# The late form of attention starts at unit 16 instead of unit 24, inside the first batch

## The chip, the cores and the metric

The kernel runs on one core of one Trainium2 chip. Its time is the device time of one execution in microseconds; lower is better. The core has five engines that work side by side, each in its own fixed order: PE (TensorE, matrix products), DVE (VectorE), ACT (ScalarE), POOL (GpSimd) and SP (SyncE, which issues nearly all DMAs here). An instruction starts when the ones before it in its engine's queue have started and what it waits for is done, so an engine can stand still behind one instruction that waits.

## The reference

Sliding-window attention with ALiBi-like distances, then a feed-forward block with a rational activation:

```
scores = q @ k^T / sqrt(64); keep = key < 8  or  0 <= query - key < 96
bias   = -slope(head) * distance                  # slopes 2^-1 .. 2^-8
attn   = softmax(keep ? scores + bias : -1e9) @ v # 4 batches, 8 heads, 768 rows, 64 wide
x      = attn, heads side by side                 # 3072 tokens x 512
h      = x @ w_in                                 # 512 -> 2048
g      = (a0 + a1 h + a2 h^2 + a3 h^3) / (1 + |b0| |h| + |b1| h^2 + 1e-6)
out    = g @ w_out                                # 2048 -> 512
```

## The kernel before

**Units and pairs.** The tokens go in 12 chunks of 256, a chunk is two tiles of 128 rows, a batch is six tiles. A *unit* is one tile and one pair of heads, so a chunk has 8 units, a batch 24, and the program 96 (`u`, or `t` for the step of the loop that starts it). A tile sees itself and the tile before it (window 96) and the first 8 keys of the batch. A *pair* `f` is a chunk's FFN on two blocks of 128 hidden columns: 8 pairs per chunk, 96 in all. Step `t` starts unit `t` and the pair `f` whose `turn(f)` falls on it: the FFN lags the attention by 10 steps at first and by 13 later (EARLY_LAG, LAG).

**The plain form** (units below PLAIN = 24). q and k are transposed on PE (L390); ACT scales q into `qz` (L403) and copies k into `kF` (L405), which holds two tiles of keys, the own and the former. The scores (L434) are full fp32 products; on PE each such product appears as two records. DVE adds the mask and takes the minimum (L453), ACT exponentiates (L463), DVE forms the reciprocal sums (L468, L470), POOL normalizes (L479). The probabilities are transposed on PE (L492) and copied out by ACT, from unit 21 on by DVE (L493). L541 multiplies with v; `st_x` splits the result into a rounded part and a rest (L570 ACT, L571 DVE).

**The late form** (units from PLAIN on). q and k of two units are moved by a DMA into a ring of one buffer, `moved` (L148, tiles `mv`), and transposed with a rounding type (L384). ACT writes the rounded half and DVE the rest of keys and queries into `kq` (L416, L417), two DMAs build the swapped query `qT` (L421, L422), and the score takes four faster matmuls (L439). The normalized probabilities are transposed in 32x32 blocks by DVE (L504), written to DRAM and read back by five DMAs (L507, L515). Here a unit's score comes two steps after its start and its product with v eight steps after; v is loaded at step `t` instead of `t - 4`.

**FFN.** The first chunk (pairs 0 to 7) uses fp32 weights (`full`, L264 and L343). The later ones use weights split in two (`hi`, `w_lo`; L272 and L348, three matmuls for each product). `split_w` makes the splits at the pairs 5 to 14 (SPLITS; L223, L224) on DVE, ACT and POOL. Weights arrive in steps 0 to 16 (WSCHED), are decoded by L203, L207, L208, L210. `h` has two buffers in PSUM, so the first matmul of pair f + 2 waits for the last reader of pair f, L304 on DVE. The elementwise steps of a pair are L296 to L298, L312, L313, L327 on ACT, L303, L304, L317 to L319 on DVE, L305 and L328 on POOL.

**What sets the order.** Each group of instructions gets a number, `base + 1000 * step + PRI[...]`, and a list scheduler puts the instructions of every engine into a fixed order by it. At `t == PLAIN` the pool `early` (kF, qz, three of the raw weight buffers) is closed and the pool `late` (kq, kG, halves, moved, turned, qT) takes its place in SBUF, so its first writes wait for the last readers of the old one. In the kernel before, this falls on the end of the first batch, where tile 0 of the next batch needs no earlier keys.

Of the kernel before, what the change touches and what calls it, by code (L numbers as in the profile page):

```python
# [9 lines left out]
F32 = mybir.dt.float32  # L10
FR = mybir.dt.float32r
# [3 lines left out]
AF = mybir.ActivationFunctionType  # L15
ALU = mybir.AluOpType
PSUM = bass.MemoryType.PSUM

P = 128
G = 8  # L20
# [6 lines left out]
LAG = 13  # L27
EARLY_LAG = 10
# [4 lines left out]
EARLY = 21  # L33


PLAIN = 24
DIVIDED = 8

WSCHED = {0: [(1, 1)], 1: [(1, 0)], 3: [(1, 3)], 4: [(1, 2)], 6: [(0, 0)], 7: [(0, 1)], 8: [(1, 5)], 9: [(1, 4)],
          10: [(0, 2)], 11: [(0, 3)], 12: [(0, 4), (1, 6)], 13: [(1, 7)], 14: [(0, 5)], 15: [(0, 6)], 16: [(0, 7)]}  # L40

SPLITS = {4: 0, 5: 2, 6: 4, 7: 8, 8: 12, 9: 16, 10: 19, 11: 22, 12: 25, 13: 28, 14: 32}

# [64 lines left out]
def tile_kernel(ctx: ExitStack, tc: tile.TileContext, q, k, v, n_global, n_local,  # L108
                w_in, w_out, ca, cb, out):
    nc = tc.nc  # L110
    B, H, S, D = q.shape
# [6 lines left out]
    NPAIR = H // 2  # L118
    UPC = 2 * NPAIR
    FPC = NFT // 2  # L120
# [4 lines left out]
    pl = SimpleNamespace(tmps=TMPS, gbufs=GBUFS, split=False)  # L125
# [5 lines left out]
    def unit(u):  # L131
        c, j = divmod(u, UPC)
        t, p = divmod(j, NPAIR)
        b, i = divmod(2 * c + t, NT)
        return c, t, p, b, i
# [238 lines left out]
    def blocks_of(x, i):  # L374
        return x if i else x[..., 0, :]

    def st_qkT(u):
        p = unit(u)[2]
        if u >= PLAIN:
            tk = pl.ps_t.tile([P, 2, 2, P], FR, tag="t", name=f"tk{u}")  # L380
# [15 lines left out]
    def st_qkE(u):  # L396
        c, t, p, b, i = unit(u)
        tk = tqk.pop(u)
        if u < PLAIN:
            qz = pl.qz[:, u % 3]  # L400
# [26 lines left out]
    def st_score(u):  # L427
# [3 lines left out]
        for x in range(2):  # L431
            h = 2 * p + x
            if u < PLAIN:
                nc.tensor.matmul(out=blocks_of(s_ps[:, x], i), lhsT=qT[:, x, :], rhs=blocks_of(pl.kF[:, p], i),  # L434
# [3 lines left out]
            for z, lhsT in enumerate((pl.kq[:, h, 2, :], qT[:, x, :])):  # L438
                nc.tensor.matmul(out=s_ps[:, x], lhsT=lhsT, rhs=rhs, start=(z == 0), stop=(z == 1))  # L439
        if 1 <= i < NT - 1 and u < PLAIN:  # L440
            nc.gpsimd.tensor_copy(out=pl.kF[:, p, i % 2, 0:G], in_=pl.kGF[:, p, :])
# [4 lines left out]
        def mask(x):  # L446
            m0, m = (mask0, masks) if u < PLAIN or x == 0 else (pl.half0, pl.halves)
            return m0 if i == 0 else m[:, 0:2, :] if i % 2 else m[:, 1:3, :]
        pr = pl.att.tile([P, 2, 2, P], F32, tag="prob", name=f"pr{u}")
        st = stats[:, u % 4]  # L450
        for x in range(2):
            h = 2 * p + x
            nc.vector.tensor_tensor_reduce(  # L453
                out=blocks_of(pr[:, x], i), in0=blocks_of(s_ps[:, x], i), in1=mask(x),
                scale=-(2.0 ** -(h + 1 if u < PLAIN else 2 * p + 1)), scalar=3e38, op0=ALU.add, op1=ALU.min, accum_out=st[:, x:x + 1])
        prob[u] = (pr, st)
# [120 lines left out]
    def windowed(lates):  # L577
# [32 lines left out]
        base = tc.cur_priority  # L610

        def halve_masks():
            for m, full_m in ((pl.halves, masks), (pl.half0, mask0)):
                nc.vector.tensor_scalar(out=m, in0=full_m, scalar1=0.5, scalar2=None, op0=ALU.mult)

        def turn(f):
            return f + EARLY_LAG + (LAG - EARLY_LAG) * min(max(f - 2 * FPC, 0), FPC) / FPC

        f = -1
        for t in range(NU + LAG + F2 + 1):  # L620
            step = int(turn(f + 1)) <= t
            f += step
            when = {True: 1000 * turn(f), False: 1000 * t}
            pri = {True: PRI_A if f < FPC else PRI, False: PRI_A if t < FPC + EARLY_LAG else PRI}

            def on(name, fn, u, *args, ffn=False, more=0):
                if 0 <= u < NU:
                    tc.cur_priority = int(base + when[ffn] + pri[ffn][name] + more)
                    fn(u, *args)

            def ffn(name, fn, u, *args):
                if step:
                    on(name, fn, u, *args, ffn=True)
# [15 lines left out]
            for u in behind(1):  # L649
                on("score", st_score, u)  # L650
                on("soft", st_soft, u)
                on("sums", st_sums, u)
            if t == PLAIN:
                scope.close()
                pl.late = lates.enter_context(tc.tile_pool(name="late", bufs=1))
                pl.kq = pl.late.tile([P, H, 3, P], FR, name="kq")
                pl.kG = pl.late.tile([P, H, G], FR, name="kG")
                pl.halves = pl.late.tile([P, 3, P], BF16, name="halves")
                pl.half0 = pl.late.tile([P, P], BF16, name="half0")
                tc.cur_priority = base + 1000 * t  # L660
                halve_masks()
                on("split", st_move, t)
            ffn("ffn1a", st_ffn1, f, 0)
            if t < PLAIN or t % 2 == 0:
# [138 lines left out]
    with ExitStack() as es:  # L803
        pl.far = es.enter_context(tc.tile_pool(name="far", bufs=1, space=bass.MemoryType.DRAM))
        pl.ldp = es.enter_context(tc.tile_pool(name="ldp", bufs=2))
        pl.att = es.enter_context(tc.tile_pool(name="att", bufs=2))
        pl.ffn = es.enter_context(tc.tile_pool(name="ffn", bufs=2))
        pl.ps_h = es.enter_context(tc.tile_pool(name="ps_h", bufs=2, space=PSUM))
        pl.ps_o = es.enter_context(tc.tile_pool(name="ps_o", bufs=2, space=PSUM))
        pl.ps_r = es.enter_context(tc.tile_pool(name="ps_r", bufs=1, space=PSUM))  # L810
        pl.ps_t = es.enter_context(tc.tile_pool(name="ps_t", bufs=3, space=PSUM))
        with ExitStack() as lates:
            windowed(lates)
# [53 lines left out]
```

## Time and profile before

| | |
|---|---|
| median of 3 runs | 733.48 us (733.4 to 734.27) |
| the profiled execution | 732.77 us, span 730.9 us, mean granted clock 0.995 |
| busy in the span | PE 706.0 us (97%), PE weight loads 608.0 (83%), DVE 604.1 (83%), ACT 577.1 (79%), POOL 457.5 (63%) |
| chain that ended last | PE 83%, DVE 6%, ACT 5%, DMA 2%, issue 2% |

The span runs from the first to the last instruction of the profiled execution; the execution's own time is 1.87 us longer. Busy time is a union: where two rows of an engine overlap, the time counts once, while the durations in a row's own column run into the next row. A matmul's row is longer than the time until the next matmul starts, since they are pipelined. The chain of waits is followed back from the last instruction, and each of its pieces lasts until the next piece begins. A few matmul records can be missing.

### The profile page before, as it was taken

Reading aid. Unit: us, or ns where it says so; the run is one execution under the profiler, and the core shown is the slowest. Engines: PE = TensorE matmul, PEld = TensorE weight load, DVE = VectorE, ACT = ScalarE, POOL = GpSimd, SP = SyncE. Lnnn points to the kernel's source line nnn. Section 1 sums busy time; section 2 is a strip of 40 time slices with the busy share of each in tenths; the row PEclk is TensorE's granted clock in tenths of the full one; section 3 lists DMA queues with packets and bytes.
Section 4 is the critical chain, followed back from the end, with each engine's and each line's share of the span. In section 5 each row is a group of like instructions: output and inputs, shape, how many; then the busy total and the mean of one; then the engine's idle time right before and its main releaser. Section 6 shows DMA issues by size and latency. Waiting matters only on the chain.

```text
span 730.9 us, 14868 instructions
## 1 busy us (share of the span) xinstructions
PE 706.0 (97%) x4762; PEld 608.0 (83%) x4762; DVE 604.1 (83%) x1508; ACT 577.1 (79%) x1304; POOL 457.5 (63%) x504
## 2 busy tenths in 40 slices
PE   5898999999999999999999999999999999999996
PEld 4575666788978889988988998998998998988894
DVE  5789966789889898888889889898889988875664
ACT  6798576977988788888887878887888878865764
POOL 3275986767567675665566657665667666754441
PEclk9999999999999999999999999999999999999998
DMA  9987210114564654645536455665346454421001
GB/s 265 294 278 215 89 23 22 52 23 105 157 166 133 200 154 130 182 141 154 142 111 181 140 136 166 173 183 137 98 121 197 138 160 129 118 88 30 30 1 34
DMA packets 139899, 96.76 MB, mean 132 GB/s; under 512 B 84260, under 2 KB 124196, under 8 KB 139812
## 3 DMA queue, kind: packets, MB, share of 16 engines
q1 hardware_dynamic: 138608, 95.20, 45.4%
q8 instruction: 40, 0.66, 0.4%
q10 hardware_dynamic: 1204, 0.52, 0.3%
q14 instruction: 47, 0.39, 0.2%
HBM read 53.22 MB, written 23.59 MB: 105 GB/s over the span
## 4 chain that ended last, share of the span: by engine, by line
PE 83%; DVE 6%; ACT 5%; DMA 2%; issue 2%; POOL 0%; SPq 0%; DVEq 0%; ACTq 0%; POOLq 0%
PE h L272 32%; PE acc L348 32%; PE o L541 5%; PE s L439 4%; PE acc L343 2%; PE h L264 2%; PE s L434 2%; DMA r<-in_moe_w_in_dram 1%; ACT pr L463 1%; PE tk L384 1%; PE tp L492 1%; DVE fu L303 1%; DVE fu L319 1%; DVE pr L453 1%; DMA nat<-in_q_dram 1%
## 5 line engine op out<-in xcount | busy, mean ns | idle before, releaser
L272 PE MATMUL h<-xh,win_l 128*128 128x256 f32 x704 | 197.1, 280 | 0.0
L479 POOL TENSOR_SCALAR pr<-pr,stats 128x256 f32<-128x256 f32 (+1 forms) x176 | 156.2, 898 | 59.5 <-DVE stats L470 37.0
L305 POOL TENSOR_TENSOR fa<-fa,fs 128x512 f32<-128x512 f32 x95 | 123.7, 1302 | 92.0 <-ACT fs L298 86.5
L348 PE MATMUL acc<-wout_l,g 128*128 128x512 f32 x352 | 139.3, 396 | 0.0
L328 POOL TENSOR_TENSOR g<-fu,g 128x512 fp32r<-128x512 f32 x87 | 113.9, 1309 | 33.9 <-ACT g L327 31.1
L272 PEld LDWEIGHTS h<-xh,win_l 128*128 128x128 f32 x704 | 133.2, 189 | 1.8 <-issue 0.5
L463 ACT ACTIVATE pr<-pr,stats 128x256 f32<-128x256 f32 (+1 forms) x192 | 93.1, 488 | 18.5 <-DVE stats L453 17.2
L296 ACT ACTIVATE fu<-h,coef 128x512 f32<-128x512 f32 (+1 forms) x97 | 74.9, 772 | 39.5 <-PE h L272 34.5
L317 DVE SCALAR_TENSOR_TENSOR fu<-fu,coef,q 128x512 f32<-128x512 f32 (+1 forms) x97 | 71.4, 736 | 32.5 <-ACT q L313 30.6
L312 ACT ACTIVATE fs<-fa,coef 128x512 f32<-128x512 f32 (+1 forms) x97 | 69.6, 717 | 22.5 <-POOL fa L305 21.1
L303 DVE TENSOR_TENSOR fu<-fu,h 128x512 f32<-128x512 f32 (+1 forms) x97 | 65.0, 671 | 21.0 <-ACT fs L298 20.7
L348 PEld LDWEIGHTS acc<-wout_l,g 128*128 128x128 f32 x352 | 66.2, 188 | 11.8
L304 DVE SCALAR_TENSOR_TENSOR fu<-fu,coef,h 128x512 f32<-128x512 f32 (+1 forms) x97 | 71.4, 736 | 1.9
L318 DVE SCALAR_TENSOR_TENSOR q<-fa,coef,q 128x512 f32<-128x512 f32 (+1 forms) x97 | 72.1, 743 | 0.0
L417 DVE SCALAR_TENSOR_TENSOR kq<-tk,kq 64x256 fp32r<-64x256 f32 x144 | 60.6, 422 | 10.9 <-ACT kq L416 6.7
L416 ACT ACTIVATE kq<-tk 64x256 fp32r<-64x256 f32 x144 | 54.2, 376 | 19.2 <-DVE kq L417 13.6
L297 ACT ACTIVATE fa<-h,coef 128x512 f32<-128x512 f32 (+1 forms) x97 | 65.6, 676 | 1.4 <-DMA out_dram<-o 1.3
L298 ACT ACTIVATE fs<-h,coef 128x512 f32<-128x512 f32 (+1 forms) x97 | 66.2, 682 | 0.3 <-DVE q L318 0.2
L319 DVE SCALAR_TENSOR_TENSOR fu<-q,fu 128x512 f32<-128x512 f32 (+1 forms) x97 | 65.2, 672 | 1.3
L327 ACT CAST g<-fu 128x512 fp32r<-128x512 f32 (+1 forms) x89 | 54.9, 616 | 13.3 <-DVE fu L319 12.2
L504 DVE STREAM_TRANSPOSE tb<-pr 128x256 f32<-128x256 f32 (+1 forms) x144 | 58.7, 414 | 5.7 <-POOL pr L479 2.0
L313 ACT ACTIVATE q<-fs 128x512 f32<-128x512 f32 (+1 forms) x97 | 57.3, 591 | 2.0 <-DVE stats L470 0.6
(257 smaller groups left out, 1943.8 us busy)
## 6 DMA issues: line engine op xcount, KB each, us to landing
put<-tb SPq DMA_DIRECT2D x30, 512.0 KB
pT<-put SPq DMA_DIRECT2D x120, 128.0 KB
mv<-nat SPq DMA_DIRECT2D x36, 256.0 KB
qT<-kq SPq DMA_DIRECT2D x144, 64.0 KB
r<-in_moe_w_in_dram SPq DMA_DIRECT2D x16, 512.0 KB
r<-in_moe_w_out_dram SPq DMA_DIRECT2D x16, 512.0 KB
nat<-in_q_dram SPq DMA_DIRECT2D x48, 128.0 KB
vt<-in_v_dram SPq DMA_DIRECT2D x48, 128.0 KB
```

Of the source, the lines that this page charges most:

```text
L272: nc.tensor.matmul(out=hps[f][:, y, :], lhsT=w[:, fs], rhs=x[:, ct, :], start=(n == 0), stop=(n == 3 * NCT - 1))
L296: nc.scalar.activation(out=u, in_=h, func=AF.Identity, scale=a3, bias=a2)
L303: nc.vector.tensor_tensor(out=u, in0=u, in1=h, op=ALU.mult)
L304: nc.vector.scalar_tensor_tensor(out=u, in0=u, scalar=a1, in1=h, op0=ALU.add, op1=ALU.mult)
L305: side(f).tensor_tensor(out=a, in0=a, in1=s, op=ALU.add)
L317: nc.vector.scalar_tensor_tensor(out=u, in0=u, scalar=a0, in1=r, op0=ALU.add, op1=ALU.mult)
L318: nc.vector.scalar_tensor_tensor(out=r, in0=a, scalar=q1, in1=r, op0=ALU.add, op1=ALU.mult)
L319: nc.vector.scalar_tensor_tensor(out=u, in0=r, scalar=2.0, in1=u, op0=ALU.subtract, op1=ALU.mult, reverse0=True)
L328: side(f).tensor_tensor(out=g[:, 1, ys], in0=u, in1=g[:, 0, ys], op=ALU.subtract)
L348: nc.tensor.matmul(out=acc, lhsT=gs[f][:, z, y, ts], rhs=w, start=(ft == 0 and n == 0), stop=(ft == NFT - 1 and n == 2))
L463: nc.scalar.activation(out=d, in_=d, func=AF.Exp, scale=-1.0, bias=st[:, x:x + 1], accum_out=st[:, 2 + 2 * x:3 + 2 * x])
L479: nc.gpsimd.tensor_scalar(out=d, in0=d, scalar1=st[:, 6 + x:7 + x], scalar2=None, op0=ALU.mult)
```

## The change

PLAIN becomes 16. Units 16 to 23 (tiles 4 and 5 of the first batch) take the late form. Tile 4 needs the keys of tile 3, which lie in `kF` in the plain form, in a pool that is being closed. So they are written to DRAM (`kept`), read back into the one buffer of the ring `moved` (`was`), and split from there into `kq` by eight copies on ACT and eight operations on DVE (`keep_keys`, L625 and L626 of the new kernel); the columns of the first 8 keys, which kF holds already, are copied to `kG`. The growth of the lag from 10 to 13 is moved from pairs 16 to 24 to pairs 8 to 16, and the last two weight pieces are fetched and decoded at step 15.

```diff
-PLAIN = 24
+PLAIN = 16
-          10: [(0, 2)], 11: [(0, 3)], 12: [(0, 4), (1, 6)], 13: [(1, 7)], 14: [(0, 5)], 15: [(0, 6)], 16: [(0, 7)]}
+          10: [(0, 2)], 11: [(0, 3)], 12: [(0, 4), (1, 6)], 13: [(1, 7)], 14: [(0, 5)], 15: [(0, 6), (0, 7)]}
...
+        def keep_keys(kept):
+            was = pl.late.tile([P, 2, 4, D], FR, tag="moved", name="was").bitcast(F32)
+            was = was.rearrange("p z a d -> p (z a d)")[:, 0:NPAIR * P].rearrange("p (n s) -> p n s", s=P)
+            nc.sync.dma_start(out=was, in_=kept)
+            for p in range(NPAIR):
+                half = float(2.0 ** (p - 1))
+                for x in range(2):
+                    own, other = slice(x * D, (x + 1) * D), slice((1 - x) * D, (2 - x) * D)
+                    at, raw = pl.kq[:, 2 * p + x, 1, :], was[own, p, :]
+                    nc.scalar.activation(out=at[own], in_=raw, func=AF.Copy, scale=half)
+                    nc.vector.scalar_tensor_tensor(out=at[other], in0=raw, scalar=half, in1=at[own], op0=ALU.mult,
+                                                   op1=ALU.subtract)
+            nc.gpsimd.tensor_copy(out=pl.kG, in_=pl.kq[:, :, 1, 0:G])
...
         def turn(f):
-            return f + EARLY_LAG + (LAG - EARLY_LAG) * min(max(f - 2 * FPC, 0), FPC) / FPC
+            return f + EARLY_LAG + (LAG - EARLY_LAG) * min(max(f - FPC, 0), FPC) / FPC
...
             if t == PLAIN:
+                tc.cur_priority = int(base + 1000 * t - 900)
+                kept = pl.far.tile([P, NPAIR, P], F32, tag="kept", name="kept")
+                nc.sync.dma_start(out=kept, in_=pl.kF[:, :, 1, :])
                 scope.close()
...
                 halve_masks()
+                tc.cur_priority = int(base + 1000 * t - 850)
+                keep_keys(kept)
                 on("split", st_move, t)
```

On PE, the place where the late form starts. Before, around the first late transposes (`tk_1816`, units 24 and 25; `acc` is the second FFN product of pairs of the second chunk, `tp` the probabilities of a plain unit):

```order
L384 MATMUL tk_1816<-ident_r,mv_1801 128x128 x4
L348 MATMUL acc_0_1455<-w_8h,g_1732 128x512
L348 MATMUL acc_0_1455<-w_9h,g_1732 128x512
L348 MATMUL acc_0_1455<-wout_l,g_1732 128x512
L348 MATMUL acc_0_1455<-w_9h,g_1732 128x512
L492 MATMUL tp_1878<-ident,pr_1680 128x128 x4
L348 MATMUL acc_1_1469<-w_8h,g_1732 128x512
L348 MATMUL acc_1_1469<-w_9h,g_1732 128x512
```

Of the change, from its first late transposes on (`tk_1107`, units 16 and 17; `tp_1152` and `tp_1192` are plain units 14 and 15, `acc` is the fp32 product of the first chunk, `h_1242` and `h_1334` are pairs 8 and 9):

```order
L384 MATMUL tk_1107<-ident_r,mv_1100 128x128 x4
L492 MATMUL tp_1152<-ident,pr_958 128x128 x4
L492 MATMUL tp_1192<-ident,pr_1062 128x128 x4
L272 MATMUL h_1242<-xh_697,win_l 128x256
L272 MATMUL h_1242<-xh_697,w_1_0h 128x256
L272 MATMUL h_1242<-xl_698,w_1_0h 128x256
L272 MATMUL h_1242<-xh_697,win_l 128x256
L343 MATMUL acc_0_763<-w_12f,fu_1137 128x512
L343 MATMUL acc_0_763<-w_13f,fu_1137 128x512
L343 MATMUL acc_1_773<-w_11f,fu_985 128x512
L343 MATMUL acc_1_773<-w_12f,fu_1137 128x512
L343 MATMUL acc_1_773<-w_13f,fu_1137 128x512
```

The start of the late form has moved from the second chunk's FFN back into the first chunk's, and 19 rows of PE (these, six of `h_1334` and two of L541) now stand between `tk` and the first late score.

On DVE, from the first elementwise step of pair 8 (L303, `fu_1251` before, `fu_1293` in the change) to about that of pair 9 (`fu_1333`, `fu_1364`). Before:

```order
L303 TENSOR_TENSOR fu_1251<-fu_1251,h_1215 128x512
L304 SCALAR_TENSOR_TENSOR fu_1251<-fu_1251,coef,h_1215 128x512
L468 TENSOR_REDUCE stats<-stats 128x2
L470 RECIPROCAL stats<-stats 128x2
L224 TENSOR_TENSOR wout_l<-w_5f,w_5h 128x512
L223 CAST w_6h<-w_6f 128x512
L317 SCALAR_TENSOR_TENSOR fu_1251<-fu_1251,coef,q_1316 128x512
L318 SCALAR_TENSOR_TENSOR q_1316<-fa_1252,coef,q_1316 128x512
L303 TENSOR_TENSOR fu_1333<-fu_1333,h_1297 128x512
```

Of the change (`tb_1439<-pr_1327` are the 32x32 transposes of unit 17, `pr_1412` the mask step of unit 18):

```order
L303 TENSOR_TENSOR fu_1293<-fu_1293,h_1242 128x512
L453 ISA pr_1412,stats<-s_1406,masks 128x256
L453 ISA stats 128x1
L453 ISA pr_1412,stats<-s_1406,halves 128x256
L453 ISA stats 128x1
L224 TENSOR_TENSOR win_l<-w_1_2f,w_1_2h 128x512
L504 STREAM_TRANSPOSE tb_1439<-pr_1327 128x2x4x32
L304 SCALAR_TENSOR_TENSOR fu_1293<-fu_1293,coef,h_1242 128x512
L504 STREAM_TRANSPOSE tb_1439<-pr_1327 128x2x4x32
L223 CAST w_4h<-w_4f 128x512
L303 TENSOR_TENSOR fu_1364<-fu_1364,h_1334 128x512
```

L303 and L304 of a pair, which stood together, now have a unit's masks, a weight split and a 32x32 transpose between them, and the transpose waits for POOL's norm of unit 17.

## Rows read from the trace of the kernel before

**Rows 1.** The chain of waits in order of time: start, us, engine, tile, line, count.
```profile
92.16 0.61 DVE fu L319
92.82 3.70 PE acc L343 x8
...
100.17 1.72 PE acc L343 x4
...
102.22 2.59 PE h L264 x12
104.81 0.86 PE s L434 x4
...
108.04 0.44 PE tp L492 x4
...
170.00 0.29 PE tk L384 x4
...
192.86 2.84 PE h L272 x24
...
223.93 0.93 PE acc L348 x4
...
225.10 0.95 PE s L439 x8
```
**Rows 2.** Stretches: length, busy per engine (and instructions), granted clock, DMA share, GB/s.
```profile
49.90:92.80 42.90, 38.24 (x179) 26.05 (x177) 41.07 (x79) 32.90 (x73) 33.04 (x34) 0.96 0.47 151
131.90:192.70 60.80, 60.80 (x423) 52.98 (x421) 52.65 (x124) 49.91 (x117) 43.17 (x43) 1.00 0.28 74
192.70:237.50 44.80, 43.20 (x314) 38.26 (x313) 41.39 (x114) 39.35 (x92) 29.71 (x35) 1.00 0.57 158
440.00:460.00 20.00, 19.71 (x151) 17.57 (x151) 18.99 (x51) 15.96 (x36) 13.85 (x17) 1.00 0.62 175
```
**Rows 3.** Groups by line and shape: count, busy us, mean ns, idle time before.
```profile
L417 DVE SCALAR_TENSOR_TENSOR kq<-tk,kq 64x256 fp32r<-64x256 f32 x144 | 60.6, 422 | 10.9 <-ACT kq L416 6.7
L504 DVE STREAM_TRANSPOSE tb<-pr 128x256 f32<-128x256 f32 x120 | 52.0, 437 | 3.5 <-POOL fa L305 1.5 <-DMA put<-tb 0.7 <-POOL pr L479 0.5
...
L403 ACT ACTIVATE qz<-tk 64x128 f32<-64x128 f32 x48 | 12.8, 268 | 8.3 <-PE tk L390 8.0
```
**Rows 4.** DVE in order of time, a packed stretch: start, us, instruction.
```profile
131.64 0.75 DVE L318 SCALAR_TENSOR_TENSOR q<-fa,coef,q 128x512 f32<-128x512 f32 x1
132.30 0.68 DVE L303 TENSOR_TENSOR fu<-fu,h 128x512 f32<-128x512 f32 x1
```
**Rows 5.** PE and POOL in order of time, at unit 15's score.
```profile
92.02 0.60 PE L434 MATMUL s<-kF,qz 128*128 128x256 f32 x2
...
93.55 0.19 POOL L441 COPY kF<-kGF 128x8 f32<-128x8 f32 x1
```
**Rows 6.** SP's queue in order of time, two DMAs and their waiters.
```profile
170.32 0.48 SPq L148 DMA_DIRECT2D mv<-nat  x1
172.62 0.37 SPq L142 DMA_DIRECT2D nat<-in_q_dram  x1
...
200.77 0.56 SPq L507 DMA_DIRECT2D put<-tb  x1
...
203.49 0.81 SPq L515 DMA_DIRECT2D pT<-put  x2
```
**Rows 7.** DVE and PE in order of time: pair 8, unit 24, pair 18.
```profile
126.64 0.75 DVE L304 SCALAR_TENSOR_TENSOR fu<-fu,coef,h 128x512 f32<-128x512 f32 x1
...
179.44 0.39 PE L439 MATMUL s<-kq 128*128 128x256 f32 x1
...
192.70 0.28 PE L272 MATMUL h<-xh,w_1h 128*128 128x256 f32 x1
```
**Rows 8.** Groups by line and shape, POOL's norms.
```profile
L479 POOL TENSOR_SCALAR pr<-pr,stats 128x256 f32<-128x256 f32 x152 | 142.0, 945 | 45.8 <-DVE stats L470 29.5 <-ACT q L313 6.7 <-ACT fs L298 3.6
```

## The prediction

> **What bounds the kernel now.** I read the chain of waits first. Until 92.8 us it is made of DVE pieces (decoding the weights and the first FFN elementwise steps); at 92.82 PE takes it over, and from there nearly every piece is PE [rows 1]. The stretches of busy time say the same [rows 2]: from 49.9 to 92.8 DVE is busy 41.07 of 42.9 us and PE only 38.24; from 131.9 to 192.7 PE is busy in all of 60.80, DVE in 52.65. So between these times a microsecond taken off PE is a microsecond gained, as long as nothing else becomes the limit, and DVE stands only 8.2 us below the limit in 60.8. That room is the point of this prediction, because the change takes work off PE and puts work on DVE.
>
> **What PE loses.** Units 16 to 23 change form. From the chain's pieces [rows 1], where a piece lasts until the next begins: a plain unit costs 4 score records (0.86 us), 4 transposes of the probabilities (0.44) and 2 of q and k (0.11 each, as the former). A late unit costs 4 score matmuls (8 take 0.95, so 0.48) and half of four q/k transposes (0.29 for two units). That is 1.52 against 0.62, 0.90 less per unit, 7.2 us in eight. The matmuls with v (L541) stay as they are.
>
> **What DVE gets.** Per late unit two splits (L417, 0.422 each) and two 32x32 transposes (L504, 0.437) [rows 3]: 16 of each, 13.7 us. Eight splits of the kept keys (L626, 64x128 each) have no row; the same operation on twice the columns is 0.422, so they lie between 0 and 3.4 us, and ACT's copy of this very shape, 0.268 [rows 3], is nearest: 2.1. Three copies of pT (L493, units 21 to 23) leave DVE; a 512-wide copy would be near L303's 0.68 [rows 4], so 2.0 less. Net +13.8 us of rows. Rows of a packed DVE overlap: at 131.64 an instruction of 0.75 is followed after 0.66 [rows 4], 88%, so +12.1 us of time. ACT exchanges 29 short copies (three per unit and five of pT) for 24 short ones, and has 10.9 of 60.8 us free [rows 2]: nothing. POOL gets one copy of 64 columns for the kept keys, SP two DMAs. The last two weight pieces are decoded one step earlier, and the v tiles of units 16 to 22 are loaded four steps later; I cost both at nothing. The decoding is the same work on a DVE that is the chain there anyway (without that cover, four operations of about 0.7: 2.7 us), and the late form asks for v only eight steps after its unit.
>
> **What moves.** The lag of the FFN behind the attention now grows from 10 to 13 during pairs 8 to 16 instead of 16 to 24 (a pair is one f, two blocks of 128 hidden columns). PE's total is not touched by that, but three units of attention are pulled ahead of the same pair, onto the stretch in which DVE also splits the weights. I counted DVE's order from L304 of pair 8 to L304 of pair 16: the eight pairs' five operations and the weight splits are the same, but L417 goes from 8 to 22, L504 from 4 to 21, the masks of L453 from 16 to 22. At the durations of the rows this is 70.5 us instead of 56.8, or 62.0 of packed time instead of 50.0. PE's first matmul of pair 18 needs that L304 of pair 16, because h has two buffers. On PE, what stands ahead of pair 18 shrinks by 8.0 us: 16 fp32 scores less (0.43 each), 48 transposes less (0.11), 44 score matmuls more (0.12), 24 late transposes more (0.073), and 12 matmuls of the second FFN product (0.233) pushed behind. Against 7.2 in all, 0.8 us more stands behind pair 18 than before.
>
> **The start of the late form.** The last plain score is now unit 15's; before, it begins in the 92.02 piece, and POOL's column copy after it at 93.55 [rows 5]. From there a chain without branches: kF to DRAM, DRAM to the ring, eight pairs of ACT and DVE, the move of q and k, the transposes. A DMA that waits for another shows 2.3 us from issue to issue (mv at 170.32, nat at 172.62) or 2.7 through DRAM (put 200.77, pT 203.49) [rows 6]. 93.8 + 2.7 + 2.7 + 2.2 (eight ACT copies) + about 2 (DVE's place in its queue) + 2.3 = 105.7. PE, in order, has 17 us of work between that score and these transposes (two fp32 blocks of h and eleven 512-wide products at 0.86 each), so it comes at about 110: the detour through DRAM is hidden. If each trip took a microsecond more, it would still be.
> The next link is not hidden. Before, the chain has the first late transposes at 170.00, and the first late score begins at 179.44 [rows 1, 7]: 9.4 us for splits and the qT DMAs in full queues, which PE filled with plain units and whole FFN pairs. Now 6.8 us of PE work stand between tk and the first s: eight transposes, ten h matmuls, five 0.86 products, some of L541. PE waits about 2.6 us, between 0 (if the queues are emptier) and 5. Behind that, the norms of units 16 and 17 on POOL (0.945 each, four of them [rows 8]) must be done before DVE reaches L504 and, behind it, L304 of pair 8. Score 119.4, plus masks, exp and sums of 2.2, the second unit 5 later, its first norm 1: about 128, and L304 of pair 8 ends at 128.5 instead of 127.4 [rows 7]. I give this 126.5 to 133.
>
> **The sum.** From 128.5 DVE has 62.0 us of packed work. How densely can it run? 41.39 of 44.8 (92%) where it is loaded beside a full PE, 18.99 of 20 (95%) in its best late stretch, 41.07 of 42.9 (96%) where it is itself the chain [rows 2]. I take 95%: 65.3 us, so L304 of pair 16 ends at 193.8 and pair 18 begins at 194.0, where it began at 192.70 [rows 7]: 1.3 late. With the 0.8 us behind it, the span gets 2.1 us longer. After pair 18 DVE's load per pair falls under PE's and PE sets the rest. The profiled execution took 732.77 us for a span of 730.9; I keep these 1.87 us outside the span: 732.77 + 2.1 = 734.9. The runs shown have a median of 733.48, 0.7 above the profiled one, and about 0.2% (1.5 us) is what can be told from no change: faster means under 732.0, slower over 734.95. My forecast of 735 lies on that edge.
> Both ends: packed fully, 190.5, the span is 1.4 shorter; at 92%, 195.9, it is 4.2 longer; with the start at 126.5 or 133 these become 3.4 shorter and 8.7 longer.
>
> [...] In the stretch from 131.9 the matmul row is 100%, the weight loads 52.98 of 60.8, and DVE 52.65, the same [rows 2]. [...]
>
> **The rivals.**
> PE stays the bound. Then the 7.2 us come off: 725.6, or about 727 with the wait at the start. For it: DVE has to reach 62.0 of 64 us only, idle is still in its order now, and PE's own waits after 192.7 (1.6 us in 44.8 [rows 2]) may shrink. Against it: DVE would have to be packed more densely than in any stretch of rows 2, over 60 us and while waiting for ACT and POOL in order.
> The late start stalls. Its place is the tk-to-score link and the POOL norms behind it; SP, in order, holds the kept-key DMA, and behind it the move and all loads. If L304 of pair 8 comes later than 133 and DVE, now without reserve, cannot catch up, each further microsecond lands on the end: 6 us more give 742. For it: the link took 9.6 us before, with emptier DVE. A long PE wait can also cost clock: the only stretch of rows 2 with a granted clock under 1.00 is the one in which PE waited. Against it: PE has 6.8 us of other work inside the link, and another 11 (36 matmuls of h, four 0.86 products, four units' scores) before the first block that needs L304 of pair 8.
> A tie. The pulled-forward attention is compensated, since DVE has less to do later, and what PE saves equals what it waits: 733.
>
> **How the numbers follow.** Forecast (DVE is the limit for pairs 8 to 18; its own range 732 to 740) 0.46, PE stays the bound 0.29, the start stalls 0.12, a tie 0.13. The forecast's lower end (0.13) and the tie give the same 0.26; the rest of the forecast and the stall give slower 0.45; PE as the bound gives faster 0.29. The range takes in PE bound at 727 and the stall up to 744.
>
> **What would show it.** The chain should keep DVE pieces past 92.8, up to about 195. DVE should be busy 94% or more from 129 to 194, PE should show waits for DVE (fu or kq) there. The first late score should come about 9 to 10 us after the first late transposes, near 119, and pair 18's first matmul near 194. If PE is without waits in that stretch and pair 18 begins before 188, the rival with PE bound is right. If the first late score comes after 124, the stall is. If the rows of L417 or L504 are not near 0.42 and 0.44, my count of DVE is wrong.

## The result and the profile after

The changed kernel takes 743.79 us (median of 4 runs, 743.19 to 745.14) against 733.44 for the kernel before in the same series: a ratio of 1.0145, 95% interval 1.0132 to 1.0159, slower by 10.4 us. The forecast was 735, with a range of its own from 732 to 740, so the direction was right and the amount was not. The profiled execution took 743.38 us for a span of 741.6, 10.7 us more than before.

The stretches of [rows 2], in the kernel after (length, busy time per engine with its instructions, granted clock, DMA share, GB/s), with two short ones more:
```profile
49.90:92.80 42.90, 38.88 (x179) 26.26 (x177) 40.44 (x80) 32.58 (x74) 29.67 (x32) 0.92 0.47 146
131.90:192.70 60.80, 55.72 (x386) 49.44 (x387) 56.67 (x151) 47.60 (x111) 43.19 (x46) 0.94 0.58 164
132.00:136.20 4.20, 4.20 (x23) 4.20 (x24) 4.14 (x12) 3.77 (x10) 1.50 (x2) 0.59 0.68 207
170.19:173.61 3.42, 3.42 (x15) 3.03 (x14) 3.29 (x11) 2.06 (x7) 2.37 (x4) 0.50 0.47 109
192.70:237.50 44.80, 42.20 (x296) 36.75 (x295) 40.48 (x111) 37.20 (x88) 31.22 (x37) 1.00 0.58 162
440.00:460.00 20.00, 19.37 (x149) 17.25 (x148) 16.19 (x46) 15.78 (x37) 13.43 (x15) 1.00 0.49 143
```
Between 131.9 and 192.7 PE was busy in all of 60.8 us before and is now idle for 5.1; DVE has gone from 52.65 to 56.67, 93%. What PE waits for there (tile and line, releaser, us in total, times, longest; the first of these waits lies just ahead of 131.9, the others make up the 5.1):
```profile
PE h L272 <- DVE fu L304: 2.7, 1, 2.7
PE s L439 <- DMA qT<-kq: 2.2, 2, 1.8
PE h L272 <- DVE w_3h L223: 1.4, 1, 1.4
PE acc L348 <- POOL g L328: 0.8, 1, 0.8
PE h L272 <- DVE win_l L224: 0.5, 1, 0.5
```
No wait stands out: five causes, on DVE, on POOL and in the DMA queue. The chain of waits (start, us, piece) answers to [rows 1]. From 92 to 127.9 it is PE's, as before, not DVE's as I had it. From there to 199 it was PE's alone before; now DVE has 24 us of it, PE 19, POOL 9, the DMAs of qT 7 and ACT 6:
```profile
119.56 3.63 PE acc L343 x8
...
123.66 4.25 PE h L272 x36
127.92 0.68 DVE fu L303
...
129.28 1.52 DVE win_l L224
...
131.09 0.71 DVE fu L304
...
131.93 4.59 PE h L272 x24
...
140.49 2.34 DMA qT<-kq
...
145.15 2.21 DMA qT<-kq
...
196.26 2.06 DMA qT<-kq
...
198.99 2.83 PE h L272 x24
```
To put a sum under this I split PE's time: for every matmul the time to the start of the next is taken, its 30th percentile for each kind of matmul (over both traces) counts as work, the rest as stall. From before to after, work goes from 630.3 to 623.0 us (-7.3, the forecast's 7.2); with a fixed price for each kind, that says what the program holds. Stall before 128 us stays (37.3 and 37.4); from 128 to 200 it goes from 6.9 to 20.9 (+14.0), from 200 on from 46.2 to 48.1 (+1.9). Behind the last matmul 1.9 us are added. That is 10.5 of the 10.7. So the saving on PE is there at the price of its rows, and twice its amount was lost in one stretch of 72 us.

Not all of the 14.0 is waiting. In that stretch PE shows 9.7 us without a matmul, where before it shows none, and twice it works without a gap at the lower of its two clock levels (1.2 instead of 2.4 GHz): from 132.65 to 136.06, after the wait of 2.7 us, and from 170.19 to 173.61, after waits of 0.5 and 1.4 us. The 24 matmuls of h of pair 10 take 4.59 us, most of them there, those of pair 18 at full clock 2.83 (both in the chain above). By the split the two stretches hold 3.0 us of the stall.

### The profile page after: what moved, and what is told of

It is laid out like the page before. It is cut to its first block, busy times and chain, and to the rows that moved or that the text cites. A ratio compares the mean times of both kernels' runs of the same rounds, so it can differ in the third digit from the quotient of the medians.

```text
span 741.6 us, 14981 instructions
## 1 busy us (share of the span) xinstructions
PE 706.3 (95%) x4730; PEld 607.0 (82%) x4730; DVE 614.0 (83%) x1543; ACT 576.6 (78%) x1297; POOL 454.5 (61%) x505
## 4 chain that ended last, share of the span: by engine, by line
PE 81%; DVE 6%; ACT 4%; DMA 4%; issue 2%; POOL 1%; SPq 0%; ACTq 0%; DVEq 0%; POOLq 0%
PE h L272 30%; PE acc L348 29%; PE o L541 6%; PE s L439 4%; PE h L264 4%; PE acc L343 4%; PE s L434 2%; DMA put<-tb 1%; PE tk L384 1%; DVE kq L417 1%; DMA qT<-kq 1%; ACT pr L463 1%; DMA pT<-put 1%; DMA r<-in_moe_w_out_dram 1%; DVE pr L453 1%
## 5 line engine op out<-in xcount | busy, mean ns | idle before, releaser
L328 POOL TENSOR_TENSOR g<-fu,g 128x512 fp32r<-128x512 f32 x87 | 113.0, 1299 | 21.6 <-ACT g L327 18.1
L303 DVE TENSOR_TENSOR fu<-fu,h 128x512 f32<-128x512 f32 (+1 forms) x97 | 65.3, 673 | 22.0 <-ACT fs L298 20.1
L417 DVE SCALAR_TENSOR_TENSOR kq<-tk,kq 64x256 fp32r<-64x256 f32 x160 | 67.4, 422 | 16.6 <-ACT kq L416 12.1
L416 ACT ACTIVATE kq<-tk 64x256 fp32r<-64x256 f32 x160 | 60.2, 377 | 23.2 <-DVE kq L417 15.0
L304 DVE SCALAR_TENSOR_TENSOR fu<-fu,coef,h 128x512 f32<-128x512 f32 (+1 forms) x97 | 71.2, 734 | 1.6
L504 DVE STREAM_TRANSPOSE tb<-pr 128x256 f32<-128x256 f32 (+1 forms) x160 | 65.6, 416 | 7.0 <-POOL pr L479 3.0
L298 ACT ACTIVATE fs<-h,coef 128x512 f32<-128x512 f32 (+1 forms) x97 | 66.1, 682 | 0.2
L327 ACT CAST g<-fu 128x512 fp32r<-128x512 f32 (+1 forms) x89 | 54.8, 616 | 11.0 <-DVE fu L319 10.1
```

The costliest lines, as they stand in the source:

```text
L304: nc.vector.scalar_tensor_tensor(out=u, in0=u, scalar=a1, in1=h, op0=ALU.add, op1=ALU.mult)
L328: side(f).tensor_tensor(out=g[:, 1, ys], in0=u, in1=g[:, 0, ys], op=ALU.subtract)
L417: nc.vector.scalar_tensor_tensor(out=at[other], in0=raw[own], scalar=half, in1=at[own], op0=ALU.mult, op1=ALU.subtract)
```

## The experiments

Eighteen kernels were run, each beside the kernel before on the same chip (median 732.4 to 732.9 us there); the difference to those runs is the fair measure, and the text uses it. Work and stall are those of the profiled execution, split as above. In before_pe, pin_pe and pin_both the split prices the 16 altered score matmuls like records of the fp32 product (0.216 us); from start to start they take 0.12 to 0.22, so the work of these three is up to 1.5 us less than the column says, and their stall as much more (about 1.0 of it from 128 to 200).

| kernel | us | against before | ratio, 95% | work | stall 128-200 | stall from 200 |
|---|---|---|---|---|---|---|
| before | 733.4 |  | | 630.3 | 6.9 | 46.2 |
| after | 743.8 | +10.4 | 1.0132-1.0159 | 623.0 | 20.9 | 48.1 |
| turn_only | 735.8 | +3.2 | 1.0033-1.0060 | 630.3 | 6.3 | 50.2 |
| no_kept | 741.0 | +8.4 | 1.0103-1.0144 | 623.0 | 23.1 | 42.7 |
| hi_act | 745.8 | +13.2 | 1.0170-1.0210 | 623.0 | 22.4 | 47.1 |
| plain20 | 754.2 | +21.6 | 1.0264-1.0312 | 626.6 | 22.0 | 55.1 |
| no_turn | 740.6 | +8.2 | 1.0083-1.0120 | 623.0 | 18.8 | 48.0 |
| before_dve | 746.6 | +14.1 | 1.0176-1.0210 | 630.3 | 13.5 | 53.0 |
| turn_late | 742.8 | +10.3 | 1.0126-1.0163 | 623.0 | 21.6 | 46.1 |
| score_later | 735.9 | +3.5 | 1.0032-1.0065 | 623.0 | 18.6 | 44.1 |
| before_pe | 740.4 | +8.0 | 1.0093-1.0141 | 626.9 | 8.3 | 56.1 |
| score_later_before | 742.4 | +10.0 | 1.0120-1.0154 | 630.3 | 7.3 | 55.7 |
| score_later_all | 750.0 | +17.6 | 1.0217-1.0259 | 623.0 | 18.7 | 57.6 |
| score_later_no_turn | 737.3 | +4.9 | 1.0048-1.0092 | 623.0 | 18.2 | 44.3 |
| pin_pe | 728.4 | -4.2 | 0.9930-0.9975 | 626.9 | 6.8 | 45.1 |
| pin_dve | 734.7 | +2.0 | 1.0017-1.0039 | 630.3 | 8.6 | 46.8 |
| pin_both | 733.4 | +0.8 | 1.0000-1.0022 | 626.9 | 11.9 | 45.9 |
| pin_noqt | 742.8 | +10.1 | 1.0115-1.0153 | 623.0 | 19.9 | 48.7 |
| score_later_300 | 738.8 | +5.9 | 1.0068-1.0101 | 623.0 | 19.2 | 45.5 |
| score_later_600 | 745.4 | +12.5 | 1.0146-1.0180 | 623.0 | 24.8 | 46.7 |

**First series: parts of the change.** My theory was A, the load on DVE; its rivals were B, the detour and the start, and C, the lag.

turn_only, the kernel before with `f - FPC` for `f - 2 * FPC` in turn.

> The kernel before, with nothing but the lag moved to pairs 8 to 16 (plain form kept to unit 23). Theory A (the loss is DVE's: too much work for it between pairs 8 and 18, and PE waits for it): the plain form gives DVE little, so the time stays at 733, between 731.5 and 735. Theory C (pulling three units of attention ahead is the loss, whatever their form): 740 or more, with PE waits between 116 and 199. Theory B (the detour of the kept keys and the start of the late form): as A, 733.

735.75, 3.2 more, just above the 735 that A and B allowed. In the stretch itself nothing is lost (stall 6.3); what is lost lies behind 200 us, where the work is the same as before. The lag alone does not make the 14 us.

no_kept, without the detour:
```diff
-            was = pl.late.tile(...)
...
+            nc.gpsimd.memset(pl.kq[:, :, 1, :].bitcast(F32), 0.0)
             nc.gpsimd.tensor_copy(out=pl.kG, in_=pl.kq[:, :, 1, 0:G])
```


> The changed kernel without the kept keys: both trips through DRAM, the eight ACT copies and the eight DVE splits are left out, and zeros stand in their place (so units 16 to 19 leave out the real keys of the tile behind). Theory B: the late form starts some 7 us earlier, the first late score moves from 117.5 to about 112, and most of the 10.4 us come back, 736 or less. Theory A: the detour was covered by PE's work and only the DVE work of about 2 us goes, so 741 to 743. Theory C: no change, 743 to 744.

741.04, as A had it; its runs spread from 736 to 743, and the profiled one is the fastest. Pair 10 begins at 125.8 instead of 131.9, but this is lost again later: the stall from 128 to 200 is 23.1. By the medians B is worth 2 us of the 10.4, but with that spread its interval overlaps the change's.

hi_act, `HI_V = (0, 2, 4, 6)`.

> The changed kernel with the twelve weight copies of pairs 7 to 14 that stood on DVE given to ACT (0.55 us each, 6.6 us less for DVE, 7 us more for ACT, which has 13 us idle between 131.9 and 192.7). Theory A: PE's waits there shrink by about as much, 737 to 739. Theories B and C: the waits stay, 742 to 745. If ACT becomes the next limit, it is slower than 744.

745.80, 2.8 us slower than the change: the copies taken off DVE brought nothing. A's 737 to 739 did not come, but ACT was full where it got them (busy 11.83 of 12 us from 128 to 140), the case for which the expectation itself has over 744. So this run does not decide on A.

plain20, `PLAIN = 20`, with slot 0 instead of 1 in keep_keys.

> The changed kernel with the late form from unit 20 on instead of 16: the same lag, the same detour (of the tile before unit 20), but half of the PE saving (3.6 us) and half of the added DVE work. Theory A: DVE's 12 us become 6, which fit into the 8.2 us that DVE had left, so the loss goes and 730 to 734 is left. Theory B: the stall at the start remains, only later, 738 to 744. Theory C: the lag is the same, so 744 or more (less of the saving on PE).

754.18. Here A fails, and plainly: half the load, and the worst time. The stretches in which pairs 15 and 16 stand apart (as above):
```profile
176.00:188.00 12.00, 6.87 (x27) 5.55 (x28) 11.72 (x30) 7.13 (x18) 7.93 (x9) 0.86 0.50 146
188.00:200.00 12.00, 6.54 (x45) 5.27 (x43) 7.90 (x31) 4.29 (x17) 5.28 (x9) 0.92 0.71 188
```
Pair 15 begins at 162.9 and pair 16, which needs x of units 20 to 23, at 205.1. Here it is the length of the late form's chain from unit 20 to x that counts: PE has nothing left, and even DVE is idle in the second stretch. This gave theory D, the chain through queues that each work in order.

**Second series: load against chain.**

no_turn, the put DMAs read pr instead of turned:
```diff
+        if u < 24:
...
+                nc.sync.dma_start(out=put..., in_=pr...)
...
+            return
```


> The changed kernel without DVE's 32x32 transposes of units 16 to 23 (16 of 0.44 us, 7.0 us): the probabilities go to DRAM as they are, so the turning is left out for these units. Theory A (DVE's time between 128 and 199 is what PE waits for): 5 to 7 us come back, 737 to 739. Theory D (the length of the chain from unit to unit through in-order queues, not DVE's load): only the chain of each pair of units is about 1 us shorter, 742 to 744.

740.64, 2.2 us less than the change: between the two, a third of the 7 us. The edit also makes twice as many put DMAs of half the size.

before_dve, in st_spare behind st_sums:
```diff
+                nc.vector.scalar_tensor_tensor(out=sp, in0=ident..., scalar=st[:, 6 + z % 2:7 + z % 2], in1=ident..., ...)
```


> The kernel before, with four extra DVE instructions of 128x256 (near 0.42 us, 13.4 us in all) behind the sums of each unit from 16 to 23; nothing waits for their results. It has the changed kernel's load on DVE without its late form, its lag or its PE saving. Theory A: DVE has 8.2 us left in 60.8, so packed at 88 to 95% the load is 4 to 6 us too much: 736 to 740, with PE waits for DVE before 200. Theory D: no chain is longer, so 733 to 734.5.

746.61, but the load was not what I had put down: an instruction took 0.756 us in the stretch, not 0.42 (line, engine, operation, count | busy, mean ns):
```profile
L477 DVE SCALAR_TENSOR_TENSOR sp<-ident,stats 128x256 f32<-128x256 f32 x32 | 24.2, 756 | 0.4
```
24.2 us for DVE, less the 8.2 it had free, are 16.0; the time grew by 14.1. The two numbers are near each other, but the load lies between 109 and 180 us, and of the added stall 6.6 lie between 128 and 200 and 6.8 behind 200. And this run can't tell what 13.8 us do.

score_later:
```diff
-                on("score", st_score, u)
+                on("score", st_score, u, more=400 if PLAIN <= u < 24 else 0)
```


> The changed kernel with the scores of units 16 to 23 placed 0.4 of a step later in the program (priority only), so that more of PE's work stands ahead of them. Theory D: PE's waits for qT (four, 4.1 us) shrink and 2 to 4 us come back, 740 to 742. Theory A: the waits only move to h or acc, 743 to 745.

735.94: a number in a priority, and 6.9 of the 10.4 us come back, more than D had expected, but not as D had it: PE's waits for qT from 128 to 200 are 4.7 us instead of 4.1, and of the stall 2.3 us go in that stretch and 4.0 behind 200, where the edit placed nothing. DVE has as much to do as in the change; it is packed more densely in the same 60.8 us (58.13 against 56.67):
```profile
131.90:192.70 60.80, 52.94 (x359) 46.08 (x359) 58.13 (x155) 49.45 (x116) 47.64 (x49) 0.94 0.59 160
```
turn_late, `min(max(f - FPC - 4, 0), 4) / 4`.

> The changed kernel with the lag growing from 10 to 13 over pairs 12 to 16 only. Theory C in its second form (the lag's move costs together with the late form): the first loss, pairs 9 to 12, goes, and 739 to 741 is left. Theory A: the same load has to be done by pair 16, so the loss moves behind pair 12: 743 to 746.

742.83, the same as the change: growing the lag later brought nothing.

**Third series: each half alone.**

before_pe:
```diff
+                kind = FR if u >= 16 else F32
-                nc.tensor.matmul(... lhsT=qT[:, x, :], rhs=blocks_of(pl.kF[:, p], i),
+                nc.tensor.matmul(... lhsT=qT[:, x, :].bitcast(kind), rhs=blocks_of(pl.kF[:, p], i).bitcast(kind),
```


> The kernel before with the PE saving alone: the plain scores of units 16 to 23 run in the one-pass type instead of fp32 (16 matmuls, 0.43 us to about 0.12 each, 5.0 us of PE's work), with less exact scores and nothing added to any other engine. If PE is the bound there with DVE behind it, as the forecast's first part says: 728 to 729. Theory A in its strong form (DVE is already level with PE in this stretch, as its added load showed): 731 to 733.

740.38: less work on PE, nothing added anywhere, and 8 us slower; neither side had this. Its stretches from 128 to 200, 240 to 290 and 580 to 640:
```profile
128.00:200.00 72.00, 69.93 (x491) 61.23 (x490) 63.84 (x157) 62.08 (x146) 51.02 (x52) 1.00 0.34 89
240.00:290.00 50.00, 47.49 (x346) 42.18 (x345) 43.40 (x114) 41.06 (x93) 32.17 (x37) 0.97 0.61 177
580.00:640.00 60.00, 57.56 (x406) 51.09 (x405) 46.09 (x120) 44.15 (x99) 35.93 (x38) 0.97 0.43 124
```
Much of PE's idle time lies where nothing was edited. The list scheduler (the planner of the expectations) had put the same instructions into another order. That became theory R: any edit draws a new order, and the order decides. It bears on the first two series as well: each of those kernels drew an order of its own, so a difference of a few us there does not show by itself what the edited part costs.

score_later_before, `more=400 if PLAIN <= u < 32 else 0` in the kernel before.

> Control for the priority: the kernel before with the scores of its own first late units, 24 to 31, placed 0.4 of a step later. If the place of the scores is a fault of the start of the late form in general: 727 to 731. If it only bites where DVE and the queues are as full as in the changed kernel (theory A and D together): 732 to 734.

742.42: the edit that wins 6.9 us in one kernel costs 10.0 in the other.

score_later_all, `more=400 if u >= PLAIN else 0`.

> The changed kernel with the scores of all late units 0.4 of a step later, not only of 16 to 23. PE's waits for qT after 200 us were 2 us in the changed kernel, so theory D expects 1 to 2 us less than with units 16 to 23 alone, 733.5 to 736; theory A (after pair 18 PE is the bound and covers them): the same 736.

750.00, 14 us more than score_later. PE's busy time from 300 to 640, first the change's, then this kernel's:
```profile
300.00:640.00 340.00, 339.37 (x2444) 305.58 (x2443) 292.87 (x754) 278.88 (x620) 220.08 (x240) 1.00 0.52 144
```
```profile
300.00:640.00 340.00, 331.91 (x2368) 295.08 (x2367) 285.17 (x741) 270.89 (x605) 213.42 (x235) 1.00 0.51 142
```
score_later_no_turn, both edits.

> The changed kernel with the scores of units 16 to 23 later and without the 32x32 transposes of these units (left out as before, 7.0 us of DVE). Theory A: what is left of the loss is DVE's load, so another 4 to 7 us go: 729 to 732, faster than the kernel before. Theory D: the chain is now short enough and the DVE load hidden, so 735 to 736.

737.32, not below score_later. In this order the 7 us of DVE's transposes cost nothing.

**Fourth series: the order held.** These kernels add edges that fix the order of each engine's instructions as it stands in another kernel, and no wait; the engine that copies each output tile, elsewhere the scheduler's choice, is fixed too:
```diff
+    for eng, order in ORDER.items():
...
+            tc.add_manual_dep(traced[name], last, NoSync)
+            last = name
```
pin_pe is before_pe in the order of the kernel before.

> The kernel before with the PE saving alone, as in before_pe (units 16 to 23 score in the one-pass type, 3.4 us less of PE's work by that run's rows), but with every engine's instructions held in the order of the kernel before. Theory R (what before_pe lost came from its instructions being put in another order, behind 240 us): 729 to 730.5. If DVE is already level with PE in the stretch: 731 to 733.

728.43. The same instructions on every engine as in before_pe, 12 us faster, each against its own runs of the kernel before. The 16 matmuls save 4.2 to 5.0 us by their rows (not 3.4: 0.12 to 0.22 each for two records of 0.216), and 4.2 us came off (interval 1.8 to 5.1), the PE saving in full:
```profile
128.00:200.00 72.00, 71.92 (x510) 62.87 (x510) 65.06 (x160) 63.30 (x149) 51.39 (x54) 1.00 0.37 96
240.00:290.00 50.00, 49.56 (x370) 44.88 (x370) 44.62 (x116) 42.92 (x96) 34.04 (x38) 1.00 0.56 161
580.00:640.00 60.00, 60.00 (x452) 53.98 (x451) 52.44 (x132) 48.45 (x106) 41.41 (x43) 1.00 0.48 140
```
It is also the only kernel that beats both, at the price of less exact scores in eight units.

pin_dve:
```diff
+                pl.spares = [nc.vector.transpose(out=spare, in_=ident).ins.name for _ in range(44)]
```


> The kernel before in its own order, with 44 extra 128x128 transposes on DVE (0.31 us each, 13.6 us) behind the sums of units 15 to 22; nothing reads them. It is the change's DVE load without its PE saving, its chain or its order. The forecast's arithmetic (62 us of packed work at 95% end at 191.9, pair 18 began at 192.7): 732.5 to 735. Theory D (DVE serves PE in order, so that an instruction in front of another delays PE at once, long before DVE is full): 737 to 742, with PE waits for fu or g between 128 and 240.

734.68; the 44 transposes took 13.5 us. The forecast's arithmetic gives the time, D's does not. The test is milder than meant: 17 of the 44 ran before 118 us, and DVE was busy for 60.4 us from L304 of pair 8 to that of pair 16, against 53.4 in the kernel before and 62.4 in the changed one. L304 of pair 16 ended at 192.66 and pair 18 began at 193.88, so this run does not show PE waiting for it; PE's waits between 128 and 200 are for POOL's g (1.0) and for pT (0.2).

pin_both, the edits of pin_pe and pin_dve.

> Both: the kernel before in its own order, with the PE saving of pin_pe and the DVE load of pin_dve. The forecast's arithmetic: DVE sets pair 18, and 3 us of PE's saving fall behind it, 731 to 734. Theory D: the load costs PE what pin_dve shows, less the saving: 734 to 739.

733.41, again inside the forecast's arithmetic. From 131.9 to 192.7:
```profile
131.90:192.70 60.80, 57.15 (x385) 47.97 (x385) 56.25 (x141) 47.22 (x112) 41.39 (x42) 1.00 0.28 70
```
DVE is as busy in these 60.8 us as in the changed kernel (56.25 and 56.67), and the loss is 0.8 us instead of 10.4; the clock there stays at 1.00.

pin_noqt, the changed kernel's own order held:
```diff
-            for z, lhsT in enumerate((pl.kq[:, h, 2, :], qT[:, x, :])):
+            for z, lhsT in enumerate((pl.kq[:, h, 2, :], qT[:, x, :] if u >= 24 else pl.kq[:, h, 2, :])):
```


> The changed kernel in its own order, with the second score matmul of units 16 to 23 reading the first one's keys and queries instead of qT: the qT DMAs still run, but no score waits for them (the second term of these scores is wrong). Theory D: the four waits of 4.1 us go and take some of the half-clock stretches with them: 737 to 740. Theory A: DVE stays late and the waits move to h or acc: 742 to 744.

742.75, 0.3 us better than the change: without the waits for qT of units 16 to 23 the stall in the stretch is 19.9 instead of 20.9. The edit could take less than the expectation says: of the 4.1 us only 2.2, two waits, belong to these units, and the other 1.9 to units behind 23, whose waits grew to 3.6. So the waits moved, as A had it, and the chain through qT was only removed in part.

**Fifth series: is it the later score, or another order?**

> As score_later, but 0.3 of a step instead of 0.4; the planner writes a third order. If the later score is what helps (PE reaches it when qT is there): between the two, 736 to 739. Theory R (every order the planner writes is a new draw, and 0.4 was a good one): anywhere from 734 to 746, with no relation to the amount.

> As score_later, but 0.6 of a step. If the later score is what helps: 734 to 737, since the waits for qT can only shrink. Theory R: anywhere from 734 to 746, and the two together with score_later spread by more than 3 us.

738.84 and 745.40. With 0, 0.3, 0.4 and 0.6 of a step the same work loses 10.4, 5.9, 3.5 and 12.5 us: a spread of 9, nearly the loss to be explained. The three amounts spread by more than R asked for; up to 0.4 the times also fall with the amount, so both readings keep something. At 0.6 PE has a wait of 2.2 us for pT, behind the score, and waits for qT of up to 3.6.

## Why the forecast was wrong

**The terms.** The profiled span is 8.6 us longer than the sum had it. The start has 3.3 of them, the way from L304 of pair 8 to L304 of pair 16 1.2, the step from there to pair 18 0.3, and what follows pair 18 3.8. (The sum's lower ends, 1.4 and 3.4 us shorter, leave out the 0.2 from L304 to pair 18 that its other ends have.)

**PE's saving.** Right: 7.2 forecast, 7.3 as the split prices it, 8.2 of it ahead of pair 18 (forecast 8.0). And PE was the bound before: pin_pe turned 4.2 to 5.0 us less work into 4.2 us less time.

**The weighing of the two engines.** The Trainium skill's page "Perfetto Trace Analysis", section "Identifying the Most-Contended Engine", calls matmul occupancy no good measure of how close a kernel is to roofline, and has TensorE's headroom judged by MFU (its FLOPs against the peak) and the share of weight loads. By that share PE was barely ahead of DVE (52.98 and 52.65 of 60.8), and a saving on PE might have brought little. In pin_pe, with the order held, it came in full: for what one edit is worth here, the matmul row without a gap was the right sign.

**DVE's load.** Right in its terms: L417 and L504 have the durations of [rows 3], and L626, estimated at 2.1 us, took 2.5 (columns as in [rows 3]):
```profile
L417 DVE SCALAR_TENSOR_TENSOR kq<-tk,kq 64x256 fp32r<-64x256 f32 x160 | 67.4, 422 | 16.6 <-ACT kq L416 12.1
L504 DVE STREAM_TRANSPOSE tb<-pr 128x256 f32<-128x256 f32 x136 | 59.0, 438 | 6.0 <-DMA put<-tb 2.6 <-POOL pr L479 2.3
...
L626 DVE SCALAR_TENSOR_TENSOR kq<-was,kq 64x128 fp32r<-64x128 f32 x8 | 2.5, 310 | 0.3
```
From L304 of pair 8 to that of pair 16 DVE's rows add up to 71.0 us (forecast 70.5), 62.4 busy (forecast 62.0). The same stretch of the kernel before holds 60.1 and 53.4, where I had 56.8 and 50.0, so the load grew by less than I had it. Most of such a load alone costs little: 2.0 us, or 0.8 with the PE saving (pin_dve, pin_both). The norms kept their price ([rows 8], now 940 ns).

**The detour.** Right. SP's queue, with the DMAs of [rows 6]:
```profile
94.81 0.63 SPq L670 DMA_DIRECT2D kept<-kF  x1
97.53 0.35 SPq L619 DMA_DIRECT2D was<-kept  x1
103.99 0.51 SPq L148 DMA_DIRECT2D mv<-nat  x1
```
The trips take 2.7 and 6.5 us with their work, the move is issued at 104.0 where I had 103.4 (105.7 less its 2.3), and PE comes to the first late transposes at 110.05, forecast 110. The first late score begins at 117.38, 2 us earlier than forecast.

**The start.** This step failed. "L304 of pair 8 ends at 128.5" became 131.8. I let L304 wait for POOL's norms, and against a stall I counted "another 11 (36 matmuls of h, ...)" as cover. But the norms of unit 17 were done at 129.0, and DVE came to the transpose behind them at 130.72. What L304 waited for was the rest of its own chain: 18 of the 36 matmuls are pair 8's own h (PE issues them from 123.50 on), three steps on ACT read it, then L303 on DVE. The cover was part of the chain. ACT's first and last step, POOL's norms, and DVE in order of time (start, us, instruction, idle time before it and its releaser):
```profile
125.94 0.78 ACT L296 ACTIVATE fu<-h,coef 128x512 f32<-128x512 f32 x1 [0.55 <-PE h L272]
127.19 0.69 ACT L298 ACTIVATE fs<-h,coef 128x512 f32<-128x512 f32 x1
```
```profile
127.20 1.83 POOL L479 TENSOR_SCALAR pr<-pr,stats 128x256 f32<-128x256 f32 x2
```
```profile
127.91 0.69 DVE L303 TENSOR_TENSOR fu<-fu,h 128x512 f32<-128x512 f32 x1 [1.47 <-PE h L272]
...
129.20 1.60 DVE L224 TENSOR_TENSOR win_l<-w_2f,w_2h 128x512 fp32r<-128x512 f32 x1
130.72 0.43 DVE L504 STREAM_TRANSPOSE tb<-pr 128x256 f32<-128x256 f32 x1
131.09 0.70 DVE L304 SCALAR_TENSOR_TENSOR fu<-fu,coef,h 128x512 f32<-128x512 f32 x1
```
The row of L303, like the chain above, names PE, whose matmuls of pair 9's h end at the same time; L303 starts when ACT's L298 ends, at 127.88. The kernel before, for comparison:
```profile
123.95 0.78 ACT L296 ACTIVATE fu<-h,coef 128x512 f32<-128x512 f32 x1 [1.48 <-PE h L272]
```
```profile
125.92 0.69 DVE L303 TENSOR_TENSOR fu<-fu,h 128x512 f32<-128x512 f32 x1 [0.76 <-ACT fs L298]
```
So L303 came 2.0 us later than before, because h of pair 8 came 2.0 us later, and then a unit's masks, a weight split and a transpose stood ahead of L304: 3.2 us from L303 to L304 instead of 0.7. The split took 1.60 us where the same operation takes 0.69 at 123.22; why is not shown. Before, PE still had 4.5 us of other work when L304 ended (126.64 in [rows 7], pair 10 at 131.86). Now PE has none left and waits:
```profile
128.93 0.28 PE L439 MATMUL s<-kq,qT 128*128 128x256 f32 x1
131.93 0.35 PE L272 MATMUL h<-xh,w_1h 128*128 128x256 f32 x1 [2.72 <-DVE fu L304]
```
**From there to pair 18.** Right within 1.2 us in length: 66.5 us from L304 to L304, 65.3 forecast, DVE busy for 94% of them, forecast 95%. L304 of pair 16 ends at 198.35, and pair 18 begins at 198.83, forecast 194.0. But the wait that I had there is not the one that ended last. PE stood until 198.36 before a score, for qT, and had two more matmuls to do ahead of pair 18:
```profile
198.36 0.39 PE L439 MATMUL s<-kq,qT 128*128 128x256 f32 x1 [1.04 <-DMA qT<-kq]
```
The two came within 0.01 us of each other, so that pair 18 follows this L304 as forecast is in part luck.

**Behind pair 18.** Forecast 0.8 us more, measured 4.6: 0.9 are the work pushed behind, as forecast, 1.9 lie behind the last matmul (below), and the rest is stall spread over the 500 us after it, which the sum put at nothing. That PE is busy nearly all of that time was right (339.37 of 340 from 300 to 640).

**Seen from PE.** The sum let one wait, L304 of pair 16 before pair 18, stand for all. PE's stall from 128 to 200 was 14.0 more; by the forecast, pair 18 at 194.0 with 8.0 us less ahead of it, it would have been 9.3. And the sum took it that the new order would feed PE as well as the old one. Ten other kernels with the late form from 16 on have 18.2 to 24.8 us of stall there, whatever is taken from DVE, the detour or qT. pin_both, with nearly as busy a DVE and the old order, has 11.9 to 12.9.

**The rivals.** PE as the bound (725.6 to 727) did not happen. The stall at the start named the right place and by chance nearly the right time, 742, but not the mechanism: neither the detour nor the tk-to-score link was late, and L304 of pair 8 came before the 133 that it asked for. The prediction puts that link before the change at 9.4 and at 9.6 us; the rows give 9.44.

**What stays open.** Of the 14.0 us 5 to 6 appear with load and saving alone (pin_both against before, 6.9). The other 8 to 9 have not been produced by themselves: pin_both lacks the late form's chains, its DMAs, 2 us of its DVE work and its order. The runs don't separate these: other orders for the late form from 16 on were only tried through priorities, and the best of them still lost 3.5 us. The lower clock, 3.0 us of the stall by the split, follows waits in this trace and is absent from 128 to 200 in pin_both (not every wait has it: in [rows 2] PE waited 1.6 us from 192.7 on at full clock, where the prediction has one stretch with a wait only). Whether the kernel would end sooner without it is not shown: DVE is busy for 4.14 of the 4.2 us from 132.0 on as well, and four runs of the changed kernel with mean clocks of 0.988, 0.995, 0.988 and 0.992 had spans of 741.6, 742.4, 741.3 and 743.3.

## What to carry to other kernels

When a scheduler sets the order, an edit has two effects: its work, which rows price well, and a new order, which here moved the time by 12 us for identical instructions (before_pe and pin_pe); hold the order to measure the first alone before believing either. Work that is to cover a chain must not itself be a link of that chain. Check the slack of a bound at every buffer that the slower engine gives back and at every DMA that PE waits for in its order, not only at the last one.

## What the hardware showed that was not expected

Behind the last copy of the output, which both chains end with, 5.9 us follow before and 7.8 after. Before and after:
```profile
724.34 0.69 DVE o L354
```
```profile
733.10 0.69 DVE o L354
```
In the trace after, 1.6 us of it is a gap on SP between two waits of the closing sequence (738.78 and 740.38), and the queue that loads instructions moved 9 packets there instead of 8. From the last matmul to the end the 20 profiled executions take 6.6 to 9.0 us, and it goes with the program: 6.6 to 7.4 in the eight kernels with the late form from unit 24 on, 8.3 to 9.0 in nine of the twelve others (no_kept has 7.6, plain20 6.8, no_turn 6.7). The cause is not shown; a difference of 2 us in 740 can be that.

A DVE instruction of 128x256 that reads a constant tile twice took 0.47 to 1.53 us (mean 0.756), a 128x128 transpose 0.29 to 0.31 (mean 0.308): the second is the better artificial load.
